# Attention values for two heads at a time, in the two column halves of TensorE

## The chip, the cores and the metric

The kernel runs on one core of a Trainium2 chip. The metric is the time of one execution on the device in microseconds (us); shown is the median of repeated runs. The engines are PE (TensorE, matrix products; PEld is its weight load), DVE (VectorE), ACT (ScalarE), POOL (GpSimd) and SP (SyncE, which only issues transfers here).

## The reference

Block-causal attention of 8 batches with 8 heads, 576 tokens and 64 dimensions a head, and behind it a feed-forward layer over all 4608 tokens:

```python
scores = scale * np.matmul(q, k.transpose(0, 1, 3, 2))        # 8 x 8 heads, 576 x 576
scores = np.where(block_i >= block_j, scores, -1000000000.0)  # blocks of 64 tokens
attn = softmax(scores)
x = np.matmul(attn, v)             # head after head side by side: 4608 x 512
h = x @ w_in                       # 512 x 2048
g = np.maximum(0.01 * h, h)
out = g @ w_out                    # 2048 x 512
```

## The kernel before

The work list has 72 entries: batch 0 twice over its eight heads, first tokens 0 to 319 (kind "lo"), then tokens 320 to 575 (kind "hi"), and then 56 heads of batches 1 to 7 (kind "full"). For each entry the kernel computes scores (`p_s`, for every other "lo" entry `p_h`), their row maxima and exponentials into `prow`, the row sums and the normalisation, then the transposed probabilities, and from them and the values the attention output `xr`, which holds two heads on its 128 partitions: an even head on partitions 0 to 63, an odd one on 64 to 127. Tokens that are complete go in chunks of 256 through the feed-forward layer: `ffn1` (into `p_h`) and `ffn2` (into `p_o`), 18 chunks of 8 units. The weights arrive as 64-bit words in 32 pieces and are taken apart to two float parts each by DVE, ACT and POOL (`weight_piece`, tiles `raw` and `val`) while batch 0 runs.

Batches 0 and 1 and the others differ in two ways. In batches 0 and 1 PE transposes the probabilities into `p_t`, ACT or DVE copy them into `ptf`, and the values product is in plain float32, `vf` (128 x 64) as weights and `ptf` as the moving operand; its result has 64 rows. From batch 2 on DVE transposes blocks, transfers through DRAM do the rest (`turn`), and the product takes two fp32r parts. The change touches batches 0 and 1. A plain float32 product shows as two records in the trace, each with a weight load.

`attention(i)` describes all operations of entry i with the tiles that they read and write and a rank (entry number plus a constant per stage: RL for loads, RP for preparing, RB for the second half of the scores, RT for transposes, RV for the values product, RX for its copy to `xr`); `ffn1`, `ffn2` and `weight_piece` do the same with ranks of their own (LEAD, LAG, RS, RG; OFF1, SL1, AHEAD). `Plan.run` then plays all of it through with a cost for each operation and gives every engine a fixed order of instructions: whenever an engine is free in that play, it takes the ready operation of the lowest rank. For copies and subtractions the plan also chooses the engine. So a change of a constant or of a cost can move instructions anywhere. Costs in the plan are numbers of the program, not measurements of a run.

The values product of one head is put together in `product` inside `attention` (line 664 for batches 0 and 1); `put_x` copies its result from PSUM to the 64 partitions of the head in `xr` (lines 243, 244), and line 729 adds a late piece.

Of the kernel before, what the change touches and what calls it, by code (L numbers as in the profile page):

```python
# [32 lines left out]
RAWS = 3  # L33
VALS = 3

RL = 4.061
RP = 4.197
RB = -28.409
RT = 1.437
RV = 3.061  # L40
RX = -0.167
RN = -85.761
RM = -14.933
RC = 3.633

LEAD = 2.065
LAG = 1.993
RS = -1.537
RG = 1.678
OFF1 = 0.917  # L50
SL1 = 10.392
AHEAD = 4.412

LAT = 1550
HOLD = 60.979
FILL = 235
FILLTO = -63.018


LOAD = 109  # L60
RATE = 0.449
SLOW = 8000


class Plan:
# [37 lines left out]
    def run(self):  # L103
# [13 lines left out]
        start, stream = 0, 0  # L117

        def offer(i):
            for k, choice in enumerate(self.ops[i][0]):  # L120
# [27 lines left out]
        while done < total:  # L148
# [6 lines left out]
            for e, q in ready.items():  # L155
                while q and ends[q[0][1]]:
                    heapq.heappop(q)
                if not q or free[e] > now:
                    continue
                other = {"DVE": "POOL", "POOL": "DVE"}.get(e)  # L160
                if other:
                    open_ = port[other] <= now
                    can = [x for x in q if not ends[x[1]] and (open_ or (e == "DVE" and self.ops[x[1]][0][x[2]][0] == "DVE"))]
                    if not can:
                        wake.append(port[other])
                        continue
                    x = min(can)
                    q.remove(x)
                    heapq.heapify(q)
                elif e == "PE":  # L170
                    x = heapq.heappop(q)
                    if self.ops[x[1]][4] == "long":
                        self.fill = None
                    free[e] = multiply(self.ops[x[1]][0][x[2]][1], since[x[1]])
# [12 lines left out]
                order.append(fn)  # L187
                end(i, e, moved + LAT if lag else free[e])
# [38 lines left out]
def attention_ffn(ctx: ExitStack, tc: tile.TileContext, qk: bass.AP, v: bass.AP, w_in: bass.AP, w_out: bass.AP, out: bass.AP):  # L227
# [191 lines left out]
    def attention(i):  # L419
# [169 lines left out]
        for base, c0, w, items in () if flip else tgroups[kind]:  # L589
# [8 lines left out]
            if plain_v:  # L598
                add(
                    copying(w, lambda base=base, w=w: ptf[z][:, base : base + w], lambda src=src: src, sb=False),  # L600
                    r0 + RT, [("t", x)], [("ptf", y, base)],
                )
                continue

# [12 lines left out]
        ptd = [("ptf", y, g) for g in bases] if plain_v else [k for g in bases for k in (("pth", g), ("ptl", g))]  # L617
        if flip:
            ptd = [k for a in range(4) for k in (("pth", bases[a]), ("ptl", bases[a]))]
        vkey = ("vf", z) if plain_v else "vs"  # L620
        rv, rx = r0 + RV, r0 + RX

        def place(t0, t1):
            r, d = 64 * (h % 2), h // 2
# [9 lines left out]
        def put_x(x, c, t0, t1, folded=False):  # L634
            n, dst, keys = t1 - t0, place(t0, t1), keys_of(t0, t1)
            if folded:
# [5 lines left out]
            if plain_v:  # L642
                add(copying(n, dst, lambda: p_t[x][0:64, c : c + n], sb=False), rx, [("t", x)], keys)
                return
# [6 lines left out]
        x0 = bank() if kind == "full" else None  # L651
        x1 = bank()
        if x0 is None:
            x0 = x1

        def product(dst, j, cols, half, start, stop, split=False):
            if plain_v:

                def go():
                    src, to = ptf[z][:, cols], dst[0:64]  # L660
                    if split:
                        src = ptf[z][:, 1088:1600].rearrange("p (a b) -> p a b", a=2)[:, :, 192:256]
                        to = to.rearrange("p (a b) -> p a b", a=2)
                    nc.tensor.matmul(to, vf[z][:, j], src, start=start, stop=stop)  # L664

                return 4 * RATE * (cols.stop - cols.start), go

            def go():
                if half == BOTH:
                    src = later["pt"].rearrange("p y (a c) -> p y a c", a=4)[:, :, :, cols]  # L670
                    nc.tensor.matmul(dst.rearrange("p (y a c) -> p y a c", y=2, a=4), vs[:, j, :], src, start=start, stop=stop)
                    return
                src, to = later["pt"][:, half], dst
                if flip:
                    src = src.rearrange("p (a c) -> p a c", a=4)[:, :, cols]
                    to = dst.rearrange("p (a c) -> p a c", a=4)[:, :, : cols.stop - cols.start]
                elif split:
                    src = src[:, 1088:1600].rearrange("p (a b) -> p a b", a=2)[:, :, 192:256]
                    to = dst.rearrange("p (a b) -> p a b", a=2)
                else:  # L680
                    src = src[:, cols]
                nc.tensor.matmul(to, vs[:, j, :], src, start=start, stop=stop)  # L682

            return (4 if flip else 1) * (2 if half == BOTH else 1) * RATE * (cols.stop - cols.start), go

        halves = (0,) if plain_v else (0, 1)
        last = 3 if kind == "full" else spans[kind][-1][0]
        if flip:
            b0, b1 = p_t[x0], p_t[x1]
            part = [[  # L690
                product(b1, j, slice(32 * s0, 32 * s1), y, j == 1 and y == 0, j == 3 and y == 1) for y in halves
            ] for j, s0, s1 in ((1, 0, 4), (2, 4, 8), (3, 8, 11), (4, 11, 13))]
            side = product(b0[:, :256], 0, slice(13 * 32, 14 * 32), BOTH, True, True)
            one, two, three, four = part
            add([("PE", [one[0], side, one[1]])], rv, ptd + [vkey], [("t", x0), ("t", x1)])
            add([merging(b0[:, 256:384], b0[:, :256], P)], rx, [], [("t", x0)])
            add([("PE", [two[0], four[0], two[1], four[1]] + three)], rv, ptd + [vkey], [("t", x1)])
            put_x(x0, 256, 0, 64)
            put_x(x1, 0, 64, 576, True)
            late = place(512, 576)  # L700
            for r in (0, 64):
                add(
                    [("DVE", dve(64), lambda r=r: nc.vector.tensor_add(late(), p_t[x0][r : r + 64, 320:384], late()))],
                    rx, [("t", x0)], keys_of(512, 576),
                )
            return
        values = [[
            product(p_t[x1][:, c : c + e - a], j, slice(a, e), y, j == 1 and y == 0, j == last and y == halves[-1])
            for y in halves
        ] for j, a, e, c in spans[kind]]  # L710
        if kind in ends:
            c, w = ends[kind]
            outer = [product(p_t[x0][:, :w], 0, slice(c, c + w), y, y == 0, y == halves[-1], kind == "full") for y in halves]
            if kind == "full":
                one, two, three, four = values
                values = [[y for x in zip(one + two, outer + four) for y in x], three]
                add([("PE", values[0][:4])], rv, ptd + [vkey], [("t", x0), ("t", x1)])
                values[0] = values[0][4:]
            else:
                add([("PE", outer)], rv, ptd + [vkey], [("t", x0)])  # L720
        add([("PE", [y for x in values for y in x])], rv, ptd + [vkey], [("t", x1)])
        if kind == "full":
            put_x(x0, 64, 0, 64)
        put_x(x1, 0, *tokens[kind])
        if kind == "full":
            late = place(512, 576)
            for r in (0,) if plain_v else (0, 64):
                add(
                    [("DVE", dve(64), lambda r=r: nc.vector.tensor_add(late(), p_t[x0][r : r + 64, 0:64], late()))],
                    rx, [("t", x0)], keys_of(512, 576),  # L730
                )

    def turn(i, row, pkeys):
        r0 = float(i)
# [221 lines left out]
```

## Time and profile before

| | |
|---|---|
| time, median of 3 runs (lowest to highest) | 1106.93 us (1106.71 to 1107.18) |
| profiled execution: its span, from first to last instruction | 1104.7 us |
| median minus that span | 2.2 us |
| PE busy in the span | 1075.9 us, 97% |
| DVE, ACT, POOL busy | 808.9, 685.0, 437.8 us |
| values products of batches 0 and 1 (line 664) | 112 matmuls, 224 records |

The profiled execution is known by its span; the 2.2 us around it are the difference to the timed runs. Busy time of PE counts records from start to end; records overlap, since the end of one is still under way when the next starts, so what a group of records takes from PE is read from the chain of waits, where each piece of time is counted once.

### The profile page before, as it was taken

How to read it: one execution, taken by the hardware profiler on the slowest of the kernel's cores; microseconds unless marked ns; L12 is line 12 of the kernel's file. 1: busy time of each engine (PE TensorE's matmuls, PEld its weight loads, DVE VectorE, ACT ScalarE, POOL GpSimd, SP SyncE). 2: the span in 40 equal slices, each digit the busy share in tenths (PEclk: the TensorE clock that was granted, in tenths of full speed). 3: DMA queues.
4: the chain of work that ended last, by engine and by line, in shares of the span. 5: the costliest groups of instructions: out<-in, count | busy, mean ns of one | idle time of the engine just before them, and what ended most of it. 6: DMA issues, size and time to landing. Idle time of an engine off the chain costs nothing.

```text
span 1104.7 us, 19959 instructions
## 1 busy us (share of the span) xinstructions
PE 1075.9 (97%) x6792; PEld 951.1 (86%) x6792; DVE 808.9 (73%) x2001; ACT 685.0 (62%) x1664; POOL 437.8 (40%) x371
## 2 busy tenths in 40 slices
PE   5799999999999999999999999999999999999998
PEld 4577887788888999988999999989999999999997
DVE  5999867689989998976666799898989998400000
ACT  6887776577866777654655667767676766322222
POOL 2332421035754455433523455545454444412221
PEclk9999999999999999999999999999999999999999
DMA  6766432157775766654464476667676655100000
GB/s 223 219 210 203 151 115 60 52 163 210 214 205 171 204 182 199 181 168 128 129 171 120 120 216 179 202 173 208 188 209 187 203 168 161 44 20 20 1 20 20
DMA packets 94245, 166.19 MB, mean 150 GB/s; under 512 B 9664, under 2 KB 79296, under 8 KB 94144
## 3 DMA queue, kind: packets, MB, share of 16 engines
q1 hardware_dynamic: 94144, 164.93, 50.9%
q8 instruction: 53, 0.87, 0.3%
q14 instruction: 48, 0.39, 0.1%
HBM read 111.41 MB, written 53.48 MB: 149 GB/s over the span
## 4 chain that ended last, share of the span: by engine, by line
PE 77%; DVE 11%; ACT 6%; DMA 2%; issue 2%; SPq 0%; POOL 0%; ACTq 0%; DVEq 0%; POOLq 0%
PE p_h L847 29%; PE p_o L866 29%; PE p_s L498 6%; PE p_t L682 5%; PE p_t L664 4%; ACT prow L529 2%; DVE turn L745 2%; PE p_t L594 2%; DMA ptm<-way 2%; DVE nmrec L520 2%; PE p_s L488 2%; DVE qs L471 1%; ACT prow L560 1%; DVE pt L253 1%; ACT pt L243 1%
## 5 line engine op out<-in xcount | busy, mean ns | idle before, releaser
L847 PE MATMUL p_h<-xh,wih 128*128 128x256 f32 x1152 | 323.5, 281 | 1.7 <-ACT g L854 1.7
L847 PE MATMUL p_h<-xl,wih 128*128 128x256 f32 x1152 | 320.6, 278 | 0.7 <-DVE xl L253 0.6
L847 PE MATMUL p_h<-xh,wil 128*128 128x256 f32 x1152 | 319.9, 278 | 0.0
L254 POOL TENSOR_TENSOR gl<-g,gh 128x512 fp32r<-128x512 f32 x105 | 141.9, 1351 | 423.5 <-ACT gh L243 383.0
L847 PEld LDWEIGHTS p_h<-xh,wih 128*128 128x128 f32 x1152 | 216.5, 188 | 11.3 <-ACT g L854 2.1
L847 PEld LDWEIGHTS p_h<-xl,wih 128*128 128x128 f32 x1152 | 216.9, 188 | 10.6 <-DVE xl L253 1.3
L847 PEld LDWEIGHTS p_h<-xh,wil 128*128 128x128 f32 x1152 | 216.7, 188 | 0.0
L854 ACT ACTIVATE g<-p_h 128x512 f32<-128x512 f32 x144 | 85.8, 596 | 194.9 <-PE p_h L847 186.8
L529 ACT ACTIVATE prow<-p_s,nmrec 128x576 f32<-128x576 f32 (+4 forms) x308 | 160.0, 527 | 59.6 <-DVE nmrec L520 55.2
L866 PE MATMUL p_o<-woh,gh 128*128 128x512 f32 x576 | 181.2, 396 | 0.0
L866 PE MATMUL p_o<-woh,gl 128*128 128x512 f32 x576 | 179.3, 393 | 0.0
L866 PE MATMUL p_o<-wol,gh 128*128 128x512 f32 x576 | 179.0, 392 | 0.0
L254 POOL TENSOR_TENSOR pt<-ptm,pt 128x448 fp32r<-128x448 f32 x111 | 143.1, 1299 | 21.9 <-ACT pt L243 12.6
L745 DVE STREAM_TRANSPOSE turn<-prow 128x384 f32<-128x384 f32 (+3 forms) x384 | 141.2, 397 | 7.6 <-ACT prow L560 5.7
L520 DVE TENSOR_REDUCE nmrec<-p_s 128x1 f32<-128x576 f32 (+4 forms) x308 | 137.8, 480 | 2.6
L560 ACT ACTIVATE prow<-prow,nmrec 128x320 f32<-128x320 f32 (+4 forms) x231 | 110.9, 519 | 44.4 <-DVE nmrec L545 44.1
L866 PEld LDWEIGHTS p_o<-woh,gl 128*128 128x128 f32 x576 | 108.2, 188 | 24.1
L866 PEld LDWEIGHTS p_o<-wol,gh 128*128 128x128 f32 x576 | 108.2, 188 | 23.4
L498 PE MATMUL p_s<-ks,qs 128*128 128x288 f32 (+4 forms) x616 | 107.6, 307 | 3.9 <-ACT prow L529 3.6
L498 PEld LDWEIGHTS p_s<-ks,qs 128*128 128x128 f32 x616 | 89.2, 188 | 11.7 <-ACT prow L529 7.0
L866 PEld LDWEIGHTS p_o<-woh,gh 128*128 128x128 f32 x576 | 92.5, 188 | 5.9 <-issue 3.2
L243 ACT CAST pt<-ptm 128x448 fp32r<-128x448 f32 x182 | 90.7, 567 | 3.6 <-DMA ptm<-way 3.5
(83 smaller groups left out, 1422.5 us busy)
## 6 DMA issues: line engine op xcount, KB each, us to landing
way<-turn SPq DMA_DIRECT2D x192, 224.0 KB, 2.4
ptm<-way SPq DMA_DIRECT2D x192, 224.0 KB, 4.3
qk_in<-in_qk SPq DMA_DIRECT2D x56, 576.0 KB, 4.8
out<-ob SPq DMA_DIRECT2D x35, 256.0 KB, 2.4
raw<-in_w_in SPq DMA_DIRECT2D x16, 512.0 KB, 4.3
raw<-in_w_out SPq DMA_DIRECT2D x16, 512.0 KB, 4.3
v_stage<-in_v SPq DMA_DIRECT2D x48, 160.0 KB, 2.3
qk_in<-in_qk SPq DMA_DIRECT2D x8, 320.0 KB, 4.5
```

What stands on the lines that cost most here:

```text
L243: one = lambda: nc.scalar.copy(dst(), src())
L254: ("POOL", pool2(n), lambda: nc.gpsimd.tensor_sub(dst(), one(), two())),
L498: go = lambda ap=ap, cols=cols, moving=moving, first=first, last=last: nc.tensor.matmul(ap, qs[z][:, cols], moving, start=first, stop=last)
L520: [("DVE", dve(kw[t]), lambda t=t, ap=ap, flat=flat: nc.vector.tensor_reduce(nm[z][: qn[t], at_col[t] : at_col[t] + 1], ap[: qn[t]], axis= ...
L529: nc.scalar.activation(o, ap[: qn[t]], AF.Exp, bias=nm[z][: qn[t], at_col[t] : at_col[t] + 1], scale=1.0, accum_out=sums[z][: qn[t], at_co ...
L560: ("ACT", act(kw[t], True), lambda: nc.scalar.mul(p(), p(), by)),
L664: nc.tensor.matmul(to, vf[z][:, j], src, start=start, stop=stop)
L682: nc.tensor.matmul(to, vs[:, j, :], src, start=start, stop=stop)
L745: nc.vector.transpose(dst, src.rearrange("p (s b i) -> p s b i", b=4, i=32))
L847: nc.tensor.matmul(hh[:, i, :], w[:, d, f * P : (f + 1) * P], x[:, d, :], start=k == 0, stop=k == len(terms) - 1)
L854: add([("ACT", act(512), lambda: nc.scalar.activation(g, hh, AF.Prelu, alpha=0.01))], rank, [("h", z)], ["g"])
L866: nc.tensor.matmul(p_o[m], a[:, i, m * P : (m + 1) * P], w[:, 2 * u + i, :], start=u == 0 and k == 0, stop=u == NU - 1 and k == 5,)
```

## The change

The values product of batches 0 and 1 is no longer described with each head but once for two heads, with the odd one (`paired`). A matmul of the even head writes PSUM partitions 0 to 63, the one of the odd head partitions 64 to 127 of the same bank, and they follow each other in turns. One copy then moves both heads' result over 128 partitions to `xr`. `ptf` has two buffers also in batch 0, where both heads shared one. In the plan a product of a head counts half as long as before, and each step between such products and other matmuls costs 100 ns (CHANGE). Of the constants 16 have new numbers, so the whole order is another.

```diff
-RL = 4.061
-RP = 4.197
-RB = -28.409
-RT = 1.437
-RV = 3.061
+RL = 4.464
+RP = 4.663
+RB = -34.524
+RT = 1.268
+RV = 2.091
...
+CHANGE = 100
...
-        def multiply(matmuls, at):
-            nonlocal start, stream
+        def multiply(matmuls, at, half):
+            nonlocal start, stream, halved
+            if half != halved:
+                start, stream, halved = max(start + stream + CHANGE, now), 0, half
...
-    ptf = [fixed([P, 1024], F32, "ptf", None, pool)] * 2
+    ptf = fixed([P, 1024], F32, "ptf", 2, pool)
...
+        if plain_v:
+            if z:
+                paired(b, h // 2, kind, bases, rv, rx)
+            return
...
+    def paired(b, d, kind, bases, rv, rx):
+        ptd = [("ptf", z, g) for z in range(2) for g in bases] + [("vf", z) for z in range(2)]
+
+        def product(x, c, j, a, e, start, stop, split=False):
+
+            def go(z):
+                src, to = ptf[z][:, a:e], p_t[x][64 * z : 64 * z + 64, c : c + e - a]
+                if split:
+                    src = ptf[z][:, 1088:1600].rearrange("p (a b) -> p a b", a=2)[:, :, 192:256]
+                    to = to.rearrange("p (a b) -> p a b", a=2)
+                nc.tensor.matmul(to, vf[z][:, j], src, start=start, stop=stop)
+
+            return [(2 * RATE * (e - a), lambda z=z: go(z)) for z in range(2)]
+
+        def put(x, c, t0, t1, more=False):
...
+            to, of = (lambda: xr[b % 2][:, d, t0:t1]), (lambda: p_t[x][:, c : c + t1 - t0])
...
+        add([("PE", [y for x in values for y in x])], rv, ptd, [("t", x) for x in {x0, x1} - {None}], kind="half")
+        if kind == "full":
+            put(x0, 64, 0, 64)
+        put(x1, 0, *tokens[kind])
+        if kind == "full":
+            put(x0, 0, 512, 576, True)
```

PE at the start of the program, before: the transposes of the first "lo" head end, then its four values matmuls come (line 664), then transposes of the second head (`p_t_98`, `p_t_99` are the two PSUM banks; `vf_122`, `vf_123` the values of the even and the odd head).

```order
L594 MATMUL p_t_99<-ident,prow_0_71 128x64
L594 MATMUL p_t_99<-ident,prow_2_73 128x128
L664 MATMUL p_t_99<-ptf,vf_122 64x64
L664 MATMUL p_t_99<-ptf,vf_122 64x256
L664 MATMUL p_t_99<-ptf,vf_122 64x192
L664 MATMUL p_t_99<-ptf,vf_122 64x64
L594 MATMUL p_t_98<-ident,prow_3_74 128x128
```

PE at the same place in the change (line 696 is the values product, line 597 the transposes, line 491 scores).

```order
L597 MATMUL p_t_99<-ident,prow_4_75 128x128
L491 MATMUL p_s<-qk_in_84 128x320
L491 MATMUL p_s<-qk_in_84 128x192
L491 MATMUL p_s<-qk_in_84 128x64
L696 MATMUL p_t_99<-ptf_121,vf_123 64x64
L696 MATMUL p_t_99<-ptf_122,vf_124 64x64
L696 MATMUL p_t_99<-ptf_121,vf_123 64x256
L696 MATMUL p_t_99<-ptf_122,vf_124 64x256
L696 MATMUL p_t_99<-ptf_121,vf_123 64x192
L696 MATMUL p_t_99<-ptf_122,vf_124 64x192
L696 MATMUL p_t_99<-ptf_121,vf_123 64x64
L696 MATMUL p_t_99<-ptf_122,vf_124 64x64
```

The first head's four matmuls have moved behind the transposes of the second head and the scores of the third, and alternate with the second head's; the lone groups of four are gone.

PE in batch 1, before, at the sixth of its heads: the values product stands in two pieces with scores of a later head between them (L498 scores, L866 feed-forward).

```order
L866 MATMUL p_o_102<-woh,gl_107 128x512 x2
L664 MATMUL p_t_98<-ptf_1_1259,vf_1_1261 64x512
L664 MATMUL p_t_99<-ptf_1_1259,vf_1_1261 64x128
L664 MATMUL p_t_98<-ptf_1_1259,vf_1_1261 64x448
L664 MATMUL p_t_98<-ptf_1_1259,vf_1_1261 64x192
L498 MATMUL p_s<-ks_88,qs_86 128x448
L498 MATMUL p_s<-ks_88,qs_86 128x320
L498 MATMUL p_s<-ks_88,qs_86 128x448
L498 MATMUL p_s<-ks_88,qs_86 128x320
L664 MATMUL p_t_98<-ptf_1_1259,vf_1_1261 64x320
L866 MATMUL p_o_103<-woh,gh_105 128x512 x2
```

PE in batch 1 in the change, at the fifth and sixth head (L501 scores, L840 feed-forward).

```order
L501 MATMUL p_s<-ks_87,qs_85 128x288
L696 MATMUL p_t_98<-ptf_0_1246,vf_0_1248 64x512
L696 MATMUL p_t_98<-ptf_1_1247,vf_1_1249 64x512
L696 MATMUL p_t_99<-ptf_0_1246,vf_0_1248 64x128
L696 MATMUL p_t_99<-ptf_1_1247,vf_1_1249 64x128
L696 MATMUL p_t_98<-ptf_0_1246,vf_0_1248 64x448
L696 MATMUL p_t_98<-ptf_1_1247,vf_1_1249 64x448
L696 MATMUL p_t_98<-ptf_0_1246,vf_0_1248 64x192
L696 MATMUL p_t_98<-ptf_1_1247,vf_1_1249 64x192
L696 MATMUL p_t_98<-ptf_0_1246,vf_0_1248 64x320
L696 MATMUL p_t_98<-ptf_1_1247,vf_1_1249 64x320
L840 MATMUL p_h_100<-xh,wih 128x256
```

All ten stand in one piece. Over the whole program there are 27 such pieces between other matmuls before (8 in "lo", 8 in "hi", 11 in batch 1) and 12 in the change. Ahead of the last values matmul of batch 1 stand 384 matmuls of `ffn1` and 174 of `ffn2` in both orders, and of DVE's 57 steps that put weights together (lines 399 and 404) 56 stand ahead of its 24th reciprocal (line 545) before and 54 in the change, all 57 ahead of the 28th in both.

## Rows read from the trace of the kernel before

**Rows 1.** The page: span, busy time of the engines, PE's granted clock in 40 slices.

```profile
span 1104.7 us, 19959 instructions
PE 1075.9 (97%) x6792; PEld 951.1 (86%) x6792; DVE 808.9 (73%) x2001; ACT 685.0 (62%) x1664; POOL 437.8 (40%) x371
PEclk9999999999999999999999999999999999999999
```

**Rows 2.** Busy us of each engine (instructions) in stretches of the span.

```profile
core 0: us, PE busy (x) PEld busy (x) DVE busy (x) ACT busy (x) POOL busy (x), PEclk, DMA share, GB/s
0.00:30.00 30.00, 18.44 (x73) 13.36 (x74) 18.05 (x57) 18.61 (x53) 6.90 (x24) 0.89 0.66 211
30.00:60.00 30.00, 23.33 (x135) 16.73 (x134) 27.41 (x76) 26.16 (x76) 9.88 (x8) 0.99 0.73 225
60.00:90.00 30.00, 29.54 (x178) 23.57 (x177) 27.45 (x59) 24.59 (x51) 10.09 (x7) 1.00 0.68 208
90.00:127.00 37.00, 37.00 (x218) 29.85 (x217) 35.85 (x78) 26.31 (x53) 10.18 (x7) 1.00 0.63 198
127.00:236.00 109.00, 109.00 (x668) 86.89 (x667) 75.32 (x201) 72.81 (x193) 21.03 (x22) 1.00 0.26 83
236.00:500.00 264.00, 258.56 (x1667) 234.58 (x1666) 237.62 (x588) 183.61 (x457) 136.81 (x109) 1.00 0.68 196
500.00:940.00 440.00, 439.17 (x2830) 400.53 (x2830) 371.80 (x920) 291.60 (x715) 202.60 (x164) 1.00 0.60 171
```

**Rows 3.** Chain of waits, 115 to 236 us: start, us, what.

```profile
118.51 1.38 PE p_o L866 x6
119.89 1.88 PE p_t L664 x10
121.76 1.58 PE p_o L866 x6
...
157.71 2.84 PE p_t L664 x10
160.54 1.59 PE p_o L866 x6
...
212.73 2.30 PE p_t L664 x8
215.03 0.90 PE p_s L498 x4
215.93 0.68 PE p_t L664 x2
216.61 1.59 PE p_o L866 x6
```

**Rows 4.** Chain of waits, 30 to 127 us.

```profile
37.74 1.20 PE p_t L664 x8
...
41.06 1.20 ACT prow L529 x6
...
81.19 1.69 DVE val L404
```

**Rows 5.** Timeline around one values product of batch 1, PE and its weight loads.

```profile
157.64 2.91 PE L664 MATMUL p_t<-ptf,vf 128*64 128x512 f32 x10
158.12 0.14 PEld L664 LDWEIGHTS p_t<-ptf,vf 128*64 128x64 f32 x1 [0.29 <-DVE p_s L260]
160.47 0.30 PEld L866 LDWEIGHTS p_o<-woh,gh 128*128 128x128 f32 x2 [0.49 <-issue]
```

**Rows 6.** Instructions that write xr, 0 to 236 us, and their waits.

```profile
L243 ACT COPY xr<-p_t x23: 190/366/582, 20.7 to 228.7; 64x320 f32<-64x320 f32 x6, 64x256 f32<-64x256 f32 x6, 64x64 f32<-64x64 f32 x6, 64x512 f32<-64x512 f32 x5
L244 DVE COPY xr<-p_t x9: 216/476/683, 16.3 to 191.9; 64x512 f32<-64x512 f32 x3, 64x320 f32<-64x320 f32 x2, 64x256 f32<-64x256 f32 x2, 64x64 f32<-64x64 f32 x2
  PE p_t L664: 11.0, 12
```

**Rows 7.** The values product's line 664: records, ns min/median/max, forms.

```profile
L664 PEld LDWEIGHTS p_t<-ptf,vf x224: 132/137/231, 14.3 to 228.0; 128*64 128x64 f32 x112
L664 PE MATMUL p_t<-ptf,vf x224: 219/379/643, 14.3 to 228.3; 128*64 128x256 f32 x32, 128*64 128x64 f32 x24, 128*64 128x192 f32 x24, 128*64 128x512 f32 x8
```

More of the change, by code (lines that the diff above doesn't have):

```diff
@@ L34 @@
 VALS = 3
-RL = 4.061
-RP = 4.197
-RB = -28.409
-RT = 1.437
-RV = 3.061
-RX = -0.167
+RL = 4.464
[3 more added lines that the diff above has]
+RV = 2.091
+RX = -0.371
 RN = -85.761
-RM = -14.933
-RC = 3.633
-LEAD = 2.065
+RM = -14.398
+RC = 3.448
+LEAD = 2.0
 LAG = 1.993
[L48 to L52, printed above, removed]
+RS = -1.522
+RG = 2.674
+OFF1 = 1.587
+SL1 = 10.683
+AHEAD = 4.436
 LAT = 1550
-HOLD = 60.979
+HOLD = 60.52
 FILL = 235
-FILLTO = -63.018
+FILLTO = -60.837
 LOAD = 109
+CHANGE = 100
 RATE = 0.449
@@ L116, in run @@
         order, now, moved, done = [], 0, 0, 0
-        start, stream = 0, 0
+        start, stream, halved = 0, 0, False
         def offer(i):
@@ L173, in run @@
                         self.fill = None
-                    free[e] = multiply(self.ops[x[1]][0][x[2]][1], since[x[1]])
+                    free[e] = multiply(self.ops[x[1]][0][x[2]][1], since[x[1]], self.ops[x[1]][4] == "half")
                     end(x[1], e, free[e])
@@ L600, in attention @@
                     copying(w, lambda base=base, w=w: ptf[z][:, base : base + w], lambda src=src: src, sb=False),
-                    r0 + RT, [("t", x)], [("ptf", y, base)],
+                    r0 + RT, [("t", x)], [("ptf", z, base)],
                 )
@@ L616, in attention @@
         bases = [g[0] for g in tgroups[kind]]
[L617 to L620, printed above, removed]
         rv, rx = r0 + RV, r0 + RX
+        if plain_v:
+            if z:
+                paired(b, h // 2, kind, bases, rv, rx)
+            return
+        ptd = [k for a in range(4) for k in (("pth", bases[a]), ("ptl", bases[a]))]
+        vkey = "vs"
         def place(t0, t1):
@@ L649, in put_x, with product @@
             )
[L651 to L666, printed above, removed]
+        x0, x1 = bank(), bank()
+        def product(dst, j, cols, half, start, stop):
             def go():
@@ L672, in go @@
                     return
[L673 to L681, printed above, removed]
@@ L682, in go @@
-                nc.tensor.matmul(to, vs[:, j, :], src, start=start, stop=stop)
-            return (4 if flip else 1) * (2 if half == BOTH else 1) * RATE * (cols.stop - cols.start), go
-        halves = (0,) if plain_v else (0, 1)
-        last = 3 if kind == "full" else spans[kind][-1][0]
[L688 to L710, printed above, removed]
+                src = later["pt"][:, half].rearrange("p (a c) -> p a c", a=4)[:, :, cols]
+                to = dst.rearrange("p (a c) -> p a c", a=4)[:, :, : cols.stop - cols.start]
+                nc.tensor.matmul(to, vs[:, j, :], src, start=start, stop=stop)
+            return 4 * (2 if half == BOTH else 1) * RATE * (cols.stop - cols.start), go
@@ new lines, in attention @@
+        b0, b1 = p_t[x0], p_t[x1]
+        part = [[
+            product(b1, j, slice(32 * s0, 32 * s1), y, j == 1 and y == 0, j == 3 and y == 1) for y in range(2)
+        ] for j, s0, s1 in ((1, 0, 4), (2, 4, 8), (3, 8, 11), (4, 11, 13))]
+        side = product(b0[:, :256], 0, slice(13 * 32, 14 * 32), BOTH, True, True)
+        one, two, three, four = part
+        add([("PE", [one[0], side, one[1]])], rv, ptd + [vkey], [("t", x0), ("t", x1)])
+        add([merging(b0[:, 256:384], b0[:, :256], P)], rx, [], [("t", x0)])
@@ new lines, in attention @@
+        add([("PE", [two[0], four[0], two[1], four[1]] + three)], rv, ptd + [vkey], [("t", x1)])
+        put_x(x0, 256, 0, 64)
+        put_x(x1, 0, 64, 576, True)
+        late = place(512, 576)
+        for r in (0, 64):
+            add(
+                [("DVE", dve(64), lambda r=r: nc.vector.tensor_add(late(), p_t[x0][r : r + 64, 320:384], late()))],
+                rx, [("t", x0)], keys_of(512, 576),
+            )
+    def paired(b, d, kind, bases, rv, rx):
[9 more added lines that the diff above has]
+        def put(x, c, t0, t1, more=False):
+            keys = [("x", b % 2, 2 * d + z, y) for z in range(2) for y in (0, 1) if (t0 < 320 if y == 0 else t1 > 320)]
+            to, of = (lambda: xr[b % 2][:, d, t0:t1]), (lambda: p_t[x][:, c : c + t1 - t0])
+            if more:
+                add([("DVE", dve(t1 - t0), lambda: nc.vector.tensor_add(to(), of(), to()))], rx, [("t", x)], keys)
+            else:
+                add(copying(t1 - t0, to, of, sb=False), rx, [("t", x)], keys)
+        x0 = bank() if kind == "full" else None
+        x1 = bank()
+        last = 3 if kind == "full" else spans[kind][-1][0]
+        values = [product(x1, c, j, a, e, j == 1, j == last) for j, a, e, c in spans[kind]]
@@ L711, in attention @@
         if kind in ends:
             c, w = ends[kind]
-            outer = [product(p_t[x0][:, :w], 0, slice(c, c + w), y, y == 0, y == halves[-1], kind == "full") for y in halves]
+            outer = product(x0 if kind == "full" else x1, 0, 0, c, c + w, True, True, kind == "full")
             if kind == "full":
[L715 to L718, printed above, removed]
-            else:
-                add([("PE", outer)], rv, ptd + [vkey], [("t", x0)])
@@ L721, in attention @@
-        add([("PE", [y for x in values for y in x])], rv, ptd + [vkey], [("t", x1)])
+                values = [values[0], outer, values[1], values[3], values[2]]
+            else:
+                values = [outer] + values
+        add([("PE", [y for x in values for y in x])], rv, ptd, [("t", x) for x in {x0, x1} - {None}], kind="half")
         if kind == "full":
-            put_x(x0, 64, 0, 64)
-        put_x(x1, 0, *tokens[kind])
+            put(x0, 64, 0, 64)
+        put(x1, 0, *tokens[kind])
@@ L725, in attention @@
         if kind == "full":
[L726 to L731, printed above, removed]
+            put(x0, 0, 512, 576, True)
     def turn(i, row, pkeys):
```

3 lines of the change are left out of this document (removed).

## The prediction

> **What bounds the kernel now.** I read the page first. PE is busy 97% of the 1104.7 us, at the full granted clock in nearly every slice [rows 1]. A share over the whole span does not say what one stage is worth, so I then asked for busy time by stretch [rows 2]. The reader is to see three kinds of stretch. Up to 60 us, PE is idle for 18.2 us (30 less 18.44, and 30 less 23.33): batch 0's "lo" entries, which have no feed-forward work to fill in yet. From 60 to 127 us PE has 0.5 us idle, but DVE is also nearly full, 27.45 of 30 and 35.85 of 37 us, since it puts the weights together. From 127 to 236 us, the heads of batch 1, PE is never idle, and DVE has 33.7 us and ACT 36.2 us free. After that PE idles for 5.4 us to 500 us and 0.8 us to 940 us. The chain of waits says the same: around batch 1 and the last "hi" entries it is one unbroken row of PE pieces [rows 3], while before and during the weights it goes through ACT's exponentials and DVE's weight steps too [rows 4]. So a microsecond less of PE work is a whole one in the third stretch, about half of one in the second, and little in the first. That batch 1's gain is kept to the end follows from the filler: equally much feed-forward work stands ahead of batch 1's last values in both orders, so that what is left behind it is equal too, and PE has 99.8% of the stretch to 940 us.
>
> **What the values cost now.** All 112 matmuls of line 664 (224 records, two for each) use 64 of the array's 128 columns [rows 7]. In the chain a head costs 2.84 us in batch 1 when it stands in one piece and 2.30 + 0.68 = 2.98 us in two (five heads and three), a "hi" entry 1.88 us [rows 3], a "lo" entry 1.20 us [rows 4]. Together 5 x 2.84 + 3 x 2.98 + 8 x 1.88 + 8 x 1.20 = 23.1 + 15.0 + 9.6 = 47.7 us.
> There is a second cost. Six matmuls of line 866 take 1.38 us in the chain when they follow other work of 128 columns, and 1.58 or 1.59 us right behind a values product [rows 3]. The next weight load waits there 0.49 us [rows 5]. Leaving the 64-column form thus costs 0.2 us, 27 times before and 12 times now.
> The Trainium skill says why ("TensorEngine Tiling (Array Packing)", Key Properties): a change of the tiling mode drains TensorE, a change of the tile alone does not. The 0.2 us agree with it, and by it the turns within a pair cost nothing.
>
> **The unknown: do the two halves run at once?** No two matmuls of different columns stand side by side in the trace of before, so the price of a pair has to be bounded. Below: a pair takes as long as one head. Above: as long as two, and with a price for each turn (third rival). I take the lower end, for what the rows show of the array's use: the form 128*64 leaves half of the array's columns without work, and weights of the next record are loaded while the current one streams (a 0.14 us load at 158.12 us within the product that began at 157.64 [rows 5]), so weights of the other half need no stop either. A matmul's two records use the same half and must follow each other; in turns even, even, odd, odd, the second even record can run beside the first odd one, and so on. Only the first and the last record of a pair stay alone; I take 0.15 us a pair for that (the last matmul of a head in batch 1, 320 of 1600 columns, has a record of 2.84 x 320 / 1600 / 2 = 0.28 us, those of batch 0 with 64 columns have 0.06).
> For two or three matmuls side by side the skill has a measured case ("TensorE: Matmul & The Clock Gate", Part 3): three column tiles ran 2.38 times as fast as one after the other, 79% of the ideal. By that, an estimate, two heads would run 1.59 times as fast and the 47.7 us become 30.0 instead of 25.7, so 4 us more than my sum; no run here shows it yet.
>
> **The sum.** PE work saved, stage by stage:
> "lo": 9.6 less 4 x 1.35 = 4.2, and four exits of 0.2 less (8 to 4): 5.0 us.
> "hi": 15.0 less 4 x 2.03 = 6.9, and 0.8: 7.7 us.
> Batch 1: 23.1 less 4 x 2.99 = 11.1, and seven exits less (11 to 4) 1.4: 12.5 us.
> Together 25.2 us. What of it reaches the end: in batch 1 all 12.5 (the free 33.7 us of DVE and 36.2 of ACT cover it; with neither, nothing would come). In "hi" the DVE has only 2.6 + 2.6 + 1.2 = 6.3 us idle from 30 to 127 us, and its weight steps are in the same places of the order, so the bounds are 0 and 6.3; I take 4. In "lo" the chain holds a values piece only now and then [rows 4]; bounds 0 and 5, I take 1.
> The copies to `xr` become half as many, each over 128 partitions for the time that 64 take (a copy of 512 columns has 0.58 us on ACT, 0.69 on DVE). Of 32 copies, 23 on ACT with 366 ns and 9 on DVE with 476 ns in the median, half fall away: some 6.3 us of two engines. ACT waited 11.0 us in 12 places for values to copy [rows 6]. I count it at nothing, covered by PE in batch 1, and as part of the 4 us in "hi".
> What the pairing adds: a pair waits for the probabilities of its odd head, so the even head's result comes a head later. Behind the first values matmul on PE's queue stand other matmuls, and in the change it was put behind the odd head's transposes and, in batch 1, its scores; no PE wait for `ptf` beyond the start is to be expected where filler stands between. The next even head's copy into `ptf` now waits for the whole pair; in batch 1 a head takes 109 / 8 = 13.6 us, four times what its product and copies take. The loads of `vf` wait in SP's queue for the product that reads the buffer; now both heads' wait for the pair, and the next q and k loads stand behind them, some four entries ahead of their use by the rank RL. All that at nothing, bound 3 us.
> The new order has no price that can be read from the trace; I take nothing for it, with 3 us to either side.
> 1104.7 - 12.5 - 4 - 1 = 1087.2 us of span; with the 2.2 us between the median of the timed runs and the span, 1089.4. I say 1089 us.
>
> **The rivals.**
> First, the halves do not overlap and each record follows the last. Then only the exits are saved, 1.4 us in batch 1 and some 0.4 in "hi", and the order was laid out for products half as long, so that a stall or two takes it back: 1105 us, within what can be told. Against it speaks the idle half of the array; for it, that nothing in this trace shows an overlap of two matmuls.
> Second, overlap is there but the order gives part away: the pair's wait, or DVE in the weights, so that "hi" and "lo" give nothing and batch 1 only two thirds: 1106.9 - 8.3 = 1098.6 us. DVE's 97% from 90 to 127 us speaks for it; PE's unbroken chain in batch 1 against more of it.
> Third, slower: turning from one half to the other stops the stream for the weight load, which lies beside it now. 224 records with the 137 ns of their loads [rows 7] are 30.7 us, on PE in its unbroken chain for some two thirds of them and against exits of 3.0 us: with no overlap either up to 1106.9 + 30.7 - 3.0 = 1134.6 us; with overlap, 0.1 us a record (22 us against the 22 saved) is just even, which is where it decides. Loads lie beside streams of the same half in the rows now, which speaks against it.
> The skill has a rule for this ("TensorE: Matmul & The Clock Gate", Part 3, What overlaps and what doesn't): weight loads overlap a running matmul only if the row group differs. Both halves have the same rows, so by it the third rival comes true; the loads within the product at 158 us, with equal rows too, disagree with it.
>
> **How the numbers follow.** Overlap, and most of it kept: 0.66, from 1081.7 (all 25.2 saved) to 1095. Overlap with much given away (second rival): 0.11, 1095 to 1103. No overlap (first): 0.12, 1103 to 1108. Slower (third): 0.08, 1110 to 1135. A new order that loses more than the pairing gives: 0.03, 1110. About 0.2% (2.2 us) is what a measurement of this kernel can tell from no change. Faster: 0.66 + 0.11 + 0.02 of the first rival = 0.79; same: the other 0.10 of it; slower: 0.08 + 0.03 = 0.11. The range goes from 1079 (all saved, and 3 us from the order) to 1104, which leaves out the third rival, the lost order and most of the first. The likeliest alone has 1081 to 1095.
>
> **What would show it.** Right: a pair in batch 1 takes near 3.0 us in the chain, in "hi" 2.0, in "lo" 1.35, with odd records that start while even ones run; 12 exits of 0.2 us; the stretch of batch 1 some 12 us shorter at 100% PE; PE idle grown by some 8 us up to the end of the weights, with DVE still near full; the chain after that the same. Wrong: pairs of 5.7 us in the chain (no overlap), gaps of 0.1 us or more between records (weight loads exposed), new waits of PE for `ptf` or `vf` in front of line 696, or PE idle in batch 1.

## The result: 1% slower, and the profile after

The changed kernel takes 1117.53 us (median of 4 runs, 1115.4 to 1120.71) where the kernel before took 1107.06 us (1106.71 to 1107.27) on the same chip: a ratio of 1.0095, interval 1.0076 to 1.0114. The prediction was faster, 1089 us, 1079 to 1104; it was wrong, in sign and by range. The profiled execution took 1118.93 us with a span of 1117.1 us, against [rows 1]:

```profile
span 1117.1 us, 19948 instructions
PE 1068.4 (96%) x6792; PEld 947.9 (85%) x6792; DVE 774.2 (69%) x1969; ACT 695.0 (62%) x1672; POOL 435.5 (39%) x375
PEclk8799999999999999999999999999999999999999
```

PE has less to do and the span is longer, so PE waits more. Busy time by stretch, as in [rows 2], says where:

```profile
0.00:30.00 30.00, 17.72 (x69) 12.23 (x69) 18.16 (x58) 16.48 (x49) 8.97 (x25) 0.82 0.64 205
30.00:60.00 30.00, 22.67 (x114) 14.51 (x115) 22.82 (x65) 22.35 (x66) 10.95 (x12) 0.79 0.69 208
...
127.00:236.00 109.00, 105.28 (x712) 90.93 (x711) 79.86 (x212) 75.06 (x199) 20.34 (x22) 0.95 0.29 92
236.00:500.00 264.00, 252.47 (x1611) 227.08 (x1610) 230.28 (x584) 181.91 (x449) 129.75 (x108) 1.00 0.66 188
500.00:940.00 440.00, 432.89 (x2767) 393.78 (x2766) 335.04 (x859) 295.95 (x717) 206.71 (x166) 1.00 0.59 168
```

The largest new idle times lie where the change edits no product: from 236 to 500 us PE now idles 11.5 us (5.4 before), from 500 to 940 us 7.1 us (0.8 before). And in the first 60 us the granted clock is 0.82 and 0.79 (0.89 and 0.99 before), so PE's busy time there holds less work (183 records instead of 208).

Two marks cut the span into three parts: the last DVE step that puts weights together, and the last values record of batch 1 (in a group of instructions, the last number of the time range is the start of the last one). Before and after, the weights; then the values after, beside [rows 7]:

```profile
L404 DVE SCALAR_TENSOR_TENSOR val<-raw,val x25: 661/677/1771, 15.7 to 126.6; 128x512 int32<-128x512 int32 x25
```

```profile
L407 DVE SCALAR_TENSOR_TENSOR val<-raw,val x25: 659/685/1670, 16.5 to 130.5; 128x512 int32<-128x512 int32 x25
...
L696 PE MATMUL p_t<-ptf,vf x224: 219/379/643, 19.8 to 222.7; 128*64 128x256 f32 x32, 128*64 128x64 f32 x24, 128*64 128x192 f32 x24, 128*64 128x512 f32 x8
```

| part of the span, us | before | after | difference | forecast |
|---|---|---|---|---|
| start to last weight step | 126.6 | 130.5 | +3.9 | -5 |
| from there to the last values record | 101.7 | 92.2 | -9.5 | -12.5 |
| from there to the end ("rest") | 876.4 | 894.4 | +18.0 | 0 |
| span | 1104.7 | 1117.1 | +12.4 | -17.5 |

The middle part did three quarters of what was forecast. In the chain of waits (start, us, what; a "lo" pair, a "hi" pair, then batch 1), a pair in batch 1 takes what one head took [rows 3], 2.84 us:

```profile
53.72 2.17 PE p_t L696 x16
...
70.44 1.89 PE p_t L696 x20
...
159.73 1.39 PE p_h L840 x12
...
162.75 2.84 PE p_t L696 x20
165.59 1.58 PE p_o L859 x6
...
168.75 1.39 PE p_o L859 x6
```

A "hi" pair takes 1.89 us (one head: 1.88). The "lo" pair shown takes 2.17 us, in a stretch with the granted clock 0.79. The exit of 0.2 us (1.58 against 1.39) is still paid, now 12 times.

So the cause to be found is that of the third part. Theory: the 16 new numbers order the work behind batch 1 worse, which has nothing to do with pairs. Rival: the pair itself brings the later work out of step. The other question is why the weights end later.

### The profile page after: what moved, and what is told of

Its sections match the earlier page's. It is cut to its first block, busy times and chain, and to the rows that moved or that the text cites. A ratio compares the mean times of both kernels' runs of the same rounds, so it can differ in the third digit from the quotient of the medians.

```text
span 1117.1 us, 19948 instructions
## 1 busy us (share of the span) xinstructions
PE 1068.4 (96%) x6792; PEld 947.9 (85%) x6792; DVE 774.2 (69%) x1969; ACT 695.0 (62%) x1672; POOL 435.5 (39%) x375
## 4 chain that ended last, share of the span: by engine, by line
PE 63%; DVE 17%; DMA 8%; ACT 6%; issue 3%; SPq 2%; POOL 0%; DVEq 0%; ACTq 0%; POOLq 0%
PE p_h L840 25%; PE p_o L859 23%; PE p_s L501 5%; DMA ptm<-way 5%; DVE turn L738 4%; DVE pt L256 3%; PE p_t L664 3%; DMA way<-turn 3%; PE p_t L597 2%; ACT prow L532 2%; DVE nmrec L523 2%; PE p_t L696 2%; ACT pt L246 1%; SPq L755 1%; PE p_s L491 1%
## 5 line engine op out<-in xcount | busy, mean ns | idle before, releaser
L257 POOL TENSOR_TENSOR gl<-g,gh 128x512 fp32r<-128x512 f32 x122 | 161.9, 1327 | 469.3 <-ACT gh L246 416.2
L840 PE MATMUL p_h<-xl,wih 128*128 128x256 f32 x1152 | 322.7, 280 | 7.9 <-DVE xl L256 7.6
L840 PE MATMUL p_h<-xh,wih 128*128 128x256 f32 x1152 | 325.8, 283 | 0.0
L840 PE MATMUL p_h<-xh,wil 128*128 128x256 f32 x1152 | 321.4, 279 | 0.0
L840 PEld LDWEIGHTS p_h<-xl,wih 128*128 128x128 f32 x1152 | 218.3, 189 | 20.2 <-DVE xl L256 8.6
L840 PEld LDWEIGHTS p_h<-xh,wih 128*128 128x128 f32 x1152 | 217.7, 189 | 11.2 <-issue 1.7
L840 PEld LDWEIGHTS p_h<-xh,wil 128*128 128x128 f32 x1152 | 218.4, 190 | 0.0
L523 DVE TENSOR_REDUCE nmrec<-p_s 128x1 f32<-128x576 f32 (+4 forms) x308 | 134.6, 482 | 2.6
L257 POOL TENSOR_TENSOR pt<-ptm,pt 128x448 fp32r<-128x448 f32 x85 | 108.3, 1288 | 43.6 <-ACT pt L246 28.2
L501 PE MATMUL p_s<-ks,qs 128*128 128x288 f32 (+4 forms) x616 | 107.7, 308 | 8.7 <-ACT prow L532 8.6
L501 PEld LDWEIGHTS p_s<-ks,qs 128*128 128x128 f32 x616 | 90.3, 188 | 17.0 <-ACT prow L532 13.1
L256 DVE TENSOR_TENSOR pt<-ptm,pt 128x448 fp32r<-128x448 f32 x107 | 93.9, 923 | 5.2 <-ACT pt L246 4.1
```

The costliest lines, as they stand in the source:

```text
L256: ("DVE+" if sb else "DVE", dve(n), lambda: nc.vector.tensor_sub(dst(), one(), two())),
L257: ("POOL", pool2(n), lambda: nc.gpsimd.tensor_sub(dst(), one(), two())),
L501: go = lambda ap=ap, cols=cols, moving=moving, first=first, last=last: nc.tensor.matmul(ap, qs[z][:, cols], moving, start=first, stop=last)
L523: [("DVE", dve(kw[t]), lambda t=t, ap=ap, flat=flat: nc.vector.tensor_reduce(nm[z][: qn[t], at_col[t] : at_col[t] + 1], ap[: qn[t]], axis= ...
L840: nc.tensor.matmul(hh[:, i, :], w[:, d, f * P : (f + 1) * P], x[:, d, :], start=k == 0, stop=k == len(terms) - 1)
```

## The experiments

Each kernel's time is its median, with the ratio to runs of the kernel before beside it on the same chip (medians 1104.99 to 1107.06 us). e1 to e4, e5 to e8, e9 to e12 and e13 to e16 shared a chip each, so across these groups the difference of two ratios is surer than that of two medians. "Rest" is the part from the last values record to the end, of the profiled execution. The kernel before, profiled a second time (e8_before_again), had a span of 1106.8 us instead of 1104.7 and a rest 2.4 us longer, so a difference of 2 or 3 us in a part of one profile says little.

| kernel | us | ratio (interval) | weights end | last values | rest |
|---|---|---|---|---|---|
| before | 1107.06 | 1 | 126.6 | 228.3 | 876.4 |
| after | 1117.53 | 1.0095 (1.0076 to 1.0114) | 130.5 | 222.7 | 894.4 |
| e1_pair_old_numbers | 1110.62 | 1.0048 (1.0031 to 1.0065) | 132.7 | 223.3 | 885.1 |
| e2_single_new_numbers | 1130.87 | 1.0232 (1.0212 to 1.0252) | 134.2 | 236.3 | 895.3 |
| e3_even_then_odd | 1131.54 | 1.0235 (1.0213 to 1.0258) | 134.4 | 234.3 | 896.4 |
| e4_one_number_back | 1123.26 | 1.0157 (1.0134 to 1.0181) | 132.2 | 222.4 | 898.6 |
| e5_fill_batch0 | 1109.63 | 1.0033 (1.0019 to 1.0047) | 124.3 | 226.2 | 885.0 |
| e6_pair_copies_first | 1107.23 | 1.0017 (1.0007 to 1.0027) | 131.5 | 219.9 | 883.0 |
| e7_new_front_old_rear | 1098.28 | 0.9937 (0.9921 to 0.9952) | 131.4 | 221.0 | 877.9 |
| e8_before_again | 1108.82 (one run) | – | 126.3 | 228.0 | 878.8 |
| e9_rear_values_rank | 1132.4 | 1.0243 (1.0221 to 1.0264) | 130.2 | 222.4 | 908.7 |
| e10_rear_ffn_ranks | 1121.55 | 1.0164 (1.0137 to 1.0191) | 130.7 | 223.0 | 895.4 |
| e11_copies_first | 1107.98 | 1.0028 (1.0017 to 1.0039) | 131.7 | 222.2 | 884.4 |
| e12_single_new_front | 1112.06 | 1.0066 (1.0051 to 1.008) | 135.8 | 237.8 | 874.7 |
| e13_before_rv_up | 1153.51 | 1.0428 (1.0411 to 1.0446) | 130.2 | 237.9 | 916.2 |
| e14_e7_rv_up | 1142.68 | 1.0325 (1.0304 to 1.0346) | 130.6 | 222.8 | 919.8 |
| e15_e7_rg_new | 1100.67 | 0.995 (0.9931 to 0.9969) | 130.1 | 222.3 | 878.8 |
| e16_e7_lead_rv_moved | 1144.49 | 1.0332 (1.0307 to 1.0358) | 129.8 | 222.0 | 923.4 |

**Pair or numbers.** e1 is the change with the 16 constants of before; e2 is the kernel before with the 16 new ones and no pair. Five of the 16 lines:

```diff
-RV = 2.091
+RV = 3.061
-RX = -0.371
+RX = -0.167
-LEAD = 2.0
+LEAD = 2.065
-RG = 2.674
+RG = 1.678
-OFF1 = 1.587
+OFF1 = 0.917
```

> The paired values, with the 16 constants of before. Theory 1 (the pairing saves PE time, the new numbers make an order with stalls): pairs of 2.84 us in batch 1, PE idle near the 29 us of before plus some 8 us while the weights are put together, 1085 to 1095 us. Theory 2 (the pairing itself costs: emptier PE in batch 0, a slower clock there, waits for the odd head): 1110 to 1120 us with PE idle near 49 us, as in the changed kernel.

> Values of one head at a time as before, with the 16 new constants. Theory 1: the stalls of the new order stay and 22 us of PE work come back, 1125 to 1140 us. Theory 2: the new numbers are harmless, 1102 to 1112 us.

The numbers alone cost 25 us (1.0232, e2): of the span, 7.6 us up to the last weight step, 0.4 in the middle part and 18.9 in the rest. With them, the pair gives 13 to 15 us back (e2 to the change): 3.7 up to the last weight step, 9.9 in the middle part, 0.9 in the rest. But the pair with the old numbers is 5 us slower than before as well: the middle part gains 11.1 us, the weights lose 6.1 and the rest 8.7. So what the pair is worth depends on the order that it stands in.

**Do the halves overlap?** e3 is the change with one line different: in a pair all matmuls of the even head come first, then those of the odd one.

```diff
-        add([("PE", [y for x in values for y in x])], rv, ptd, ...)
+        add([("PE", [x[z] for z in range(2) for x in values])], rv, ptd, ...)
```

> The changed kernel with the matmuls of a pair not in turns: all of the even head, then all of the odd one; no other instruction moves. If the halves run at once only in turns, a pair takes 5.5 to 5.7 us in batch 1 (2.84 now), 3.7 in the second part of batch 0 (1.89 now), and the kernel 10 to 22 us more than the changed one, 1128 to 1139 us, the less the more of it stalls cover. If the overlap does not hang on the turns, or no time is won by it, 1117 us.

Its chain of waits in batch 1:

```profile
209.00 4.72 PE p_t L696 x18
213.72 1.57 PE p_h L840 x12
```

4.72 us for two heads, against 2.84 in turns and 5.68 for two alone: without the turns most of the overlap is gone, and 14 to 15 us of time with it. In the change the 20 weight loads of the pair at 162.75 us all lie within its 2.84 us or begin as the scores ahead of it end (timeline of weight loads, two of its lines):

```profile
162.68 0.20 PEld L696 LDWEIGHTS p_t<-ptf,vf 128*64 128x64 f32 x4
...
163.59 0.36 PEld L696 LDWEIGHTS p_t<-ptf,vf 128*64 128x64 f32 x6 [0.29 <-issue]
```

**One constant back.** e4 is the change with OFF1, which shifts the weights' due times, at its value of before.

```diff
-OFF1 = 1.587
+OFF1 = 0.917
```

> The changed kernel with one constant back, OFF1 (where the weights' pieces begin) 0.917 instead of 1.587. Theory 1, for the weights: they come earlier, PE does not run dry between 120 and 140 us and its clock stays up there, 1105 to 1112 us. Theory 2, or if the loss lies behind batch 1: 1113 to 1120 us.

Neither came: the weights do not end earlier, and the whole is 6 to 7 us slower than the change.

**The clock in batch 0.** e5 is e1 with some 116 more matmuls of the identity laid into PE's gaps of the "lo" entries; nothing reads their result.

```diff
-FILLTO = -63.018
+FILLTO = 8.0
```

> As e1 (pairs, the numbers of before), with small matmuls of the identity put into PE's gaps of batch 0's first part until the feed-forward work begins; they compute nothing that is used. If the half clock that e1 showed there (0.73 from 30 to 60 us) is what makes the weights end 6 us later than before, the granted clock is near 1.0 from 20 to 60 us, the last weight step comes near 127 us instead of 133, and the time is 1102 to 1107 us. If the stage hangs on DVE and ACT whatever PE's clock, or the small matmuls only stand in the way, 1109 to 1115 us.

Stretches of e5 (busy us by engine, clock), then its group of weight steps, then the same group of e1:

```profile
0.00:30.00 30.00, 26.60 (x179) 23.43 (x180) 18.71 (x60) 20.02 (x61) 9.23 (x26) 1.00 0.73 229
30.00:60.00 30.00, 27.98 (x234) 24.13 (x232) 26.76 (x68) 22.61 (x60) 10.64 (x9) 1.00 0.71 215
127.00:236.00 109.00, 99.61 (x656) 84.72 (x654) 74.71 (x204) 67.76 (x181) 22.49 (x22) 0.94 0.29 92
```

```profile
L407 DVE SCALAR_TENSOR_TENSOR val<-raw,val x25: 661/681/1094, 16.1 to 124.3; 128x512 int32<-128x512 int32 x25
```

```profile
L407 DVE SCALAR_TENSOR_TENSOR val<-raw,val x25: 659/679/861, 15.7 to 132.7; 128x512 int32<-128x512 int32 x25
```

The clock stays at 1.00 and the weights end 8.4 us earlier than in e1: so much the low clock of batch 0 costs there (e1 had 0.73 from 30 to 60 us), as far as the filler moves nothing else. Yet the time falls by 1 to 2 us only. PE now idles 9.4 us of the stretch from 127 to 236 us (5.7 in e1), and the last values come at 226.2 us instead of 223.3: what was gained ahead was not kept.

The low clock did not come by itself: e8, the kernel before once more, has 0.94 up to 30 us and 1.00 from there to 60 us. The numbers alone (e2) bring 0.81 from 30 to 60 us, the pair alone (e1) 0.73, both 0.79.

**The end of batch 1.** The change has no gap there: its PE is busy all through from 145 to 236 us, at the clock 1.00. In e1, PE waits 2.9 us for exponentials and then 1.7 us for `xl`: it does 1.59 us of work in the 5 us from 225 us, and then runs at half clock:

```profile
225.00:230.00 5.00, 1.59 (x6) 1.07 (x7) 4.66 (x15) 4.07 (x13) 2.51 (x2) 0.84 0.29 106
230.00:235.00 5.00, 5.00 (x24) 5.00 (x25) 1.99 (x9) 1.35 (x4) 0.00 (x0) 0.50 0.78 252
```

```profile
225.68 0.48 DVE turn L738
226.16 0.57 DVE xr L247
...
227.92 1.78 POOL xl L257
...
229.74 2.72 PE p_h L840 x11
```

The chain of e1 below its two stretches says why: the first feed-forward matmul of the next chunk waits for the copy to `xr` and for the split into `xl`, and the copy stood behind a `turn` on DVE. e6 (on e1) and e11 (on e7, below) let a pair's copies go first.

```diff
-                paired(b, h // 2, kind, bases, rv, rx)
+                paired(b, h // 2, kind, bases, rv, rx - 40)
```

> As e1, with the copies of a pair's result to xr ranked ahead of all else on ACT and DVE. If PE's gap of 4.7 us at the end of batch 1 and the half clock behind it come from the result that waits in DVE's queue, the gap shrinks to 2 us or less and the time is 1104 to 1108 us. If the gap comes from too little work that is ready whatever the copies do, 1109 to 1113 us.

> As e7, with the copies of a pair's result ranked ahead of all else, as in e6, which was 3.4 us faster than e1 by it. Where the copies hold up the chunks, 1094 to 1097 us; e7 has no PE idle at the end of batch 1, so that it may also be no change, 1097 to 1100 us.

e6 gains 3.4 us on e1. The same edit on e7 loses 9.7 us, 6.5 of it in the rest. So it is no rule: in e11 PE waits 2.3 us for `xl` at the end of batch 1, where e7 has no wait; what it moved behind that was not traced.

**Front and rear apart.** e7 has the pair and the new numbers, but only for entries of batches 0 and 1 and the feed-forward work beside them (up to entry 23, counted from 0); behind, the ranks are those of before. e12 is the same without the pair.

```diff
+FRONT = (4.464, 4.663, -34.524, 1.268, 2.091, -0.371)
...
+        RL, RP, RB, RT, RV, RX = FRONT if b < TURN else (4.061, 4.197, -28.409, 1.437, 3.061, -0.167)
...
+            LEAD, LAG, RS, RG = (2.0, 1.993, -1.522, 2.674) if i < 3 * H else (2.065, 1.993, -1.537, 1.678)
```

> The changed kernel with the new numbers for batches 0 and 1 and the numbers of before from batch 2 on (ranks of the attention stages and of the feed-forward chunks). If the 18 us that the changed kernel loses behind batch 1 come from the new numbers there, the stretch behind the last values of batch 1 is 876 to 886 us long instead of 894, and the time 1100 to 1110 us. If they come from what the pairing hands over, 1114 to 1120 us.

> As e7, but with the values of one head at a time. If the pairing is worth what e2 against the changed kernel says, 1109 to 1113 us; by the full sum of saved PE work, 1118 us or more; if it is worth nothing in a good order, 1098 to 1101 us.

e7 beats both kernels: 7 us faster than before (0.9937), some 18 faster than the change, and faster than either expectation. Its first two parts are those of the change within 2 us; its rest is 877.9 us instead of 894.4, and its stretches behind batch 1 are as full as in [rows 2]:

```profile
236.00:500.00 264.00, 257.61 (x1654) 232.98 (x1653) 233.22 (x584) 180.50 (x448) 133.34 (x109) 1.00 0.65 190
500.00:940.00 440.00, 439.17 (x2833) 400.49 (x2832) 371.43 (x917) 290.30 (x712) 203.20 (x164) 1.00 0.60 173
```

So the rear's numbers cost the change 16.5 of its 18.0 us, and the rival falls: the pair, with the order of before behind it, leaves the rest as it was. Against e12 the pair is worth 14 us of time: 4.4 us of the span up to the last weight step and 12.4 in the middle part, less 3.2 in the rest.

**Which number of the rear.** On e7, each with rear values of its own; e13 is the kernel before with RV alone raised by 0.4%. RV is the rank of the values product, LEAD that of the feed-forward units, RS shifts the split into `xh` and `xl`, RG is the rank at which the activation is copied.

```diff
 e9   RV 3.061 -> 2.091
 e10  LEAD 2.065 -> 2.0, RS -1.537 -> -1.522, RG 1.678 -> 2.674
 e13  RV 3.061 -> 3.0732 (in the kernel before, everywhere)
 e14  RV 3.061 -> 3.0732
 e15  RG 1.678 -> 2.674
 e16  LEAD 2.065 -> 2.0, RV 3.061 -> 2.996
```

> As e7 (new numbers for batches 0 and 1, those of before behind), with one number of the rear new again: RV 2.091, the rank of the values products. If the 18 us behind batch 1 come from values that now go ahead of the feed-forward work, so that none is left at the ends of the batches, 1110 to 1118 us. If from another number, 1096 to 1102 us.

> As e7, with the feed-forward ranks of the rear new again (LEAD 2.0, RS -1.522, RG 2.674). If the chunks' places make the waits for xl at the ends of the batches (7.6 us of PE in the changed kernel, and the half clock behind them), 1108 to 1118 us. If it is the values' rank, 1096 to 1102 us.

> The kernel before with one number moved by 0.4%: RV 3.0732 for 3.061, so that RV less LEAD is 1.008 for 0.996. If the place of the values against the feed-forward work decides, and a step of one is an edge, 1112 to 1125 us though nothing is paired and no other number is new. If it takes larger changes, 1103 to 1109 us.

> e7 with the same 0.4% in the rear alone (RV 3.0732). By the edge, 1108 to 1122 us; without one, 1096 to 1101 us.

> e7 with RG of the rear new (2.674; the rank at which the feed-forward's activation is copied), LEAD and RV as in e7. If the loss of e10 came over the edge between RV and LEAD, 1096 to 1102 us; if from RG, 1115 to 1125 us.

> e7 with LEAD of the rear 2.0 (the new value) and RV 2.996, so that their difference stays 0.996. If only the difference counts, 1096 to 1102 us; if LEAD itself does, 1108 to 1122 us.

RG does nothing that can be told (e15). Each of the others lengthens the rest by 17 to 46 us, and the time of all five lies above the slower of the two ranges expected. The values' rank (e9) or the feed-forward ranks (e10) alone are enough for the loss of the change. In e13 a shift of 0.012 of one rank costs 47 us of time with no pair and no new number anywhere. What it moves is seen in the chain of waits of one entry each, first e7, then e13:

```profile
644.51 0.70 PE p_s L503 x4
645.21 0.24 PE p_t L666
...
645.56 1.28 PE p_t L666 x7
646.84 1.38 PE p_o L861 x6
```

```profile
642.16 0.71 PE p_s L498 x4
642.87 2.76 PE p_o L866 x12
645.63 0.23 PE p_t L682
...
646.22 0.86 PE p_s L498 x7
647.08 1.07 PE p_t L682 x6
...
652.39 2.90 POOL xl L254
...
655.34 2.71 PE p_h L847 x11
```

In e7 the values (`p_t`) follow the first scores of the entry. In e13 two pieces of feed-forward work stand between and scores interrupt the product, the values end later, and at the end of the batch there is no feed-forward work left to cover the copy to `xr` and the split into `xl` (2.90 us on POOL); PE waits for them, and its next 11 records take 2.71 us, twice the usual. The waits of PE behind 236 us (total, times, longest) in e13, in e7, before, and in the change:

```profile
PE p_s L498 <- ACT prow L529: 22.4, 22, 2.0
PE p_h L847 <- POOL xl L254: 10.4, 5, 2.6
```

```profile
PE p_s L503 <- ACT prow L534: 4.3, 6, 1.5
...
PE p_h L842 <- DVE xl L257: 0.6, 1, 0.6
```

```profile
PE p_s L498 <- ACT prow L529: 3.6, 5, 1.7
PE p_h L847 <- DVE xl L253: 0.6, 1, 0.6
```

```profile
PE p_h L840 <- DVE xl L256: 6.9, 5, 2.6
PE p_s L501 <- ACT prow L532: 6.8, 9, 2.3
```

The change has the same two waits as e13 in smaller size: for exponentials, and for `xl` at the ends of batches. From its last values record to the end PE idles 22.4 us, before 10.1: that is 12.3 of the 18.0 us, and the other 5.7 are PE time, of which 1.8 are found in the last section and the remainder was not taken apart.

All kernels with a rest below 886 us have RV 3.061 with LEAD 2.065: just above 3.0, the rank of the first scores three entries on, and below 3.065, the next entry's feed-forward unit. e9, e10, e13, e14 and e16 leave this interval on one side or the other. That it is these two edges fits all runs, but is not shown: no run crosses the lower edge by a small step with LEAD unmoved, and e10 and e16 put the feed-forward units on the very rank of the scores (3.0) as well. e16 keeps the distance of RV to LEAD, 0.996, and is slow, which shows that this distance alone is not the rule.

## Why the prediction was wrong

**The step that failed** is "The new order has no price that can be read from the trace; I take nothing for it, with 3 us to either side". Without the pair that order costs 25 us (e2), eight times the bound. In the change 18.0 us of it show behind batch 1, and e7 against the change shows that 16.5 of them come from the rear's ranks. With it fell "That batch 1's gain is kept to the end follows from the filler": equally much feed-forward work ahead of the last values does make what is left equal, but not how well it lies beside the exponentials. PE's 99.8% of [rows 2] was the merit of that order and no property of the work, and a chance of 0.03 for a new order that loses more was far too little for 16 moved constants.

The pair itself came near its forecast where the order was the same on both sides and new: 14.5 us less span from e2 to the change and 13.6 from e12 to e7, where 17.5 was forecast. In the order of before it lost 3.7 (e1).

**Overlap: right.** I allowed 0.15 us a pair for lone records; there is no such tail, the pair takes one head's 2.84 us. (The sum's four pairs of each kind make 25.5 us, not the 25.7 that stands beside the estimate of 30.0; nothing hangs on it.) The first rival (no overlap) and the third (loads exposed) fall with it. The Trainium skill's rule that a weight load overlaps a running matmul only if the row group differs ("TensorE: Matmul & The Clock Gate", Part 3, What overlaps and what doesn't) is not what these runs show: loads of both halves, with equal rows, lie beside the streams. The case that the Trainium skill measured ("TensorE: Matmul & The Clock Gate", Part 3, Measured speedup vs the span model), three column tiles 2.38 times as fast, is 79% of its ideal; the ratio here is the full 5.68 / 2.84 = 2.0 of 2. e3's 5.68 / 4.72 = 1.2 shows what becomes of it without turns.

**Batch 1: right in mechanism, too large.** 12.5 us were forecast and 9.5 measured; in the pairs of kernels with equal numbers it was 9.9 (e2 and the change), 11.1 (before and e1) and 12.4 (e12 and e7). PE was to be busy all through. In the change it is so from 145 us on, but ahead of that it idles 3.7 us, waiting for probabilities that ACT normalises (total, times, longest, 84 to 146 us; before has no wait of PE there), and from 135 to 145 us the granted clock is 0.67:

```profile
PE p_t L597 <- ACT prow L563: 3.7, 2, 3.5
```

**"hi" and "lo": wrong in sign, by the order.** I took 5 us and the weights end 3.9 us later. e2 takes this apart: the new numbers alone make them end 7.6 us later, and the pair takes 3.7 of that back (4.4 from e12 to e7), near what I took. With the numbers of before the pair made them end 6.1 us later (e1), and e5 prices the low clock there at 8.4 us, as far as its filler moves nothing else. What such a pair does in batch 0 thus depends on the order.

**Copies, `ptf`, `vf` at nothing: right for the change.** Its engine sat idle 1.5 us in all until `ptf` came in front of line 696 (3.9 us in front of line 664 before), the groups of instructions show no wait for `vf` there, and PE has no gap at the end of batch 1. In other orders it has: in e1, e4, e5, e6 and e11 PE waits there 1.7 to 2.3 us for `xl`, which needs the copy to `xr`, and in e13 1.4 us with no pair at all.

Left open: which single neighbour in the order of the rear makes it slow, why the pair and the old numbers do not fit in batch 0, and whether another set of numbers lets the pair keep more than e7's 7 us.

## What to carry to other kernels

A static order is part of the kernel: when an edit comes with new scheduling constants, price the constants as a change of their own, by running old edit with new numbers and new edit with old ones, before crediting either. Where the trace shows the bounding engine 99.8% busy, ask what covers the end of each batch: five of the six moves of the rear's ranks tried here made the rest 17 to 46 us longer. Two products that each use half of the array's columns cost here what one costs (2.84 us), as long as their matmuls follow each other in turns.

## What was not expected of the hardware

One stall cost more than itself. In the change, at 920 us, `xl` comes late, PE waits 2.62 us, and the records behind it start every 0.21 us; at full clock 12 such records take 1.39 us in the chain (159.73 us above), 0.116 us each. So PE ran at about half speed when the wait was over: the granted clock is 1.00 up to the end of the wait and 0.63 from 923.4 to 928 us. The chain, and the timeline of PE:

```profile
921.06 2.31 DVE xl L256
...
923.41 4.50 PE p_h L840 x23
```

```profile
923.41 0.57 PE L840 MATMUL p_h<-xl,wih 128*128 128x256 f32 x1 [2.62 <-DVE xl L256]
923.78 0.41 PE L840 MATMUL p_h<-xh,wil 128*128 128x256 f32 x1
923.99 0.41 PE L840 MATMUL p_h<-xh,wih 128*128 128x256 f32 x1
```

The 23 records take 4.50 us here and would take 23 x 0.116 = 2.7 us, so the stall of 2.62 us costs 1.8 us more. In e1 the granted clock behind the gap at the end of batch 1 was 0.50, the lower of the two levels, for 5 us, and in e13 0.51 for 2.8 us behind the wait at 655 us. It is no rule of every stall: behind 236 us the change has seven other waits of 1.21 to 2.35 us, and e6 has one of 2.25 us at 225 us, and in the 4 us after each of them the granted clock is 1.00. What sets these cases apart was not tried.
